# Banded attention with two feed-forward blocks: VectorE's maxima and softmax sums as one run at the head of a step

## The chip, the cores and the metric

One core of a Trainium2 chip runs the whole program. The metric is device time in microseconds for one execution. The kernel before takes 594.93 us (median of three runs, 594.91 to 594.97). The profile is of one execution of 594.9 us; its span, from the first to the last instruction, is 593.1 us, so 1.8 us lie around it.

## The reference

Two batches of 8 heads, 768 positions, head width 64; then two feed-forward blocks on 1536 tokens.

```python
def _attn_ref(q, k, v, n_global, n_local):
    scores = scale * np.matmul(q, k.transpose(0, 1, 3, 2))
    keep = is_global | is_local            # the first 8 keys, and the last 96
    scores = np.where(keep, scores - slope * dist, -1e9)
    a = np.exp(scores - max(scores)); a = a / (a.sum(-1) + 1e-9)
    return np.matmul(a, v)

x = attn_out.transpose(0, 2, 1, 3).reshape(B * S, H * D)
x = (((x @ w1) * (x @ w2)) @ w3) @ w_out
x = ((x @ w_a) * (x @ w_b)) @ w_out2
```

## The kernel before

Attention works on **blocks** (tiles) of 128 queries: 12 of them, t = 0 to 11, six for each batch. A block's keys are its own 128 and the 128 before it; the first 32 columns of the older keys are overwritten by the batch's first keys (the global ones). A block has four units of two heads, so there are 48 units, u = 4t + c. The first batch (t < 6) multiplies the keys as they are; the second (t from 6) splits keys and queries into a rounded part and a remainder: `ks` holds both parts of the keys, `qa` and `qb` those of the queries.

The order of every engine is written by hand, one **step** after another (`band_attention`, the `while` loop). Each engine works its list strictly in order. In step u stand:

- TensorE: the scores of units u and u+1 (even u; L429 in the first batch, L446 in the second), the transposition of an older unit's probabilities (L509, unit u-5, from step 16 unit u-6), the product with the values (L545; from step 16 four units at once, in the steps with u % 4 == 2), and behind these a share of the first feed-forward block (`filler`, L827 to L829).
- ScalarE: the exponentials of unit u-2 (L481), the copy of the transposed probabilities out of PSUM (L511), a block's output rounded (`store_x`, L520), the rounded keys of a later block (`band_high`, L387), and the conversion of weights (L92, L93, L118).
- VectorE: two fused passes over the scores of unit u-1, which add the bias and find the maximum (`band_max`, L463), the sums of unit u-3 (`band_norm`: an addition L492 and a reciprocal L494; from unit 16 for two units at once, in even steps), the remainder of a block's output (`store_x_low`, L527), the copy of the global keys into the block's keys (`band_global`, L413; in the first block of a batch L411 sets them aside), the remainders of the keys and of the queries of a later block (`band_low`, L399 and L402), and the weight conversion (L97, L101, L105 in one step, L127 in the next).
- GpSimd: the division by the sums (`band_norm`, L498, two instructions for each unit, released by the reciprocal) and the rounded queries of a later block (`band_high`, L388, which writes `qa`; L402 reads it).

Block work has fixed steps. For block t: L388 and L387 in step 4t-4, L399 and L402 in step 4t-3, L413 in step 4t+3. The scores of block t+1, from step 4t+4 on, read the keys that L413 writes.

Inside a step the VectorE work comes as generators (`turns`), and `feed` takes one instruction from each in turn until all are empty. Up to step 5 it first empties the generators of attention and only then starts the weight pieces. A stage that is no generator (L413, L388, L387, L520) issues its instructions where the list of turns is built, so ahead of the first maximum. A share of feed-forward work is given to each step by a count (`spent`), not by time: a step that lasts longer gets no more of it.

After attention (from about 125 us) the feed-forward blocks run to the end; the change touches nothing of them.

Of the kernel before, what the change touches and what calls it, by code (L numbers as in the profile page):

```python
# [31 lines left out]
class Emitter:  # L32
# [519 lines left out]
    def band_attention(self, filler):  # L552

        self.v, self.qs, self.sp, self.sm, self.pt, self.pv = ({} for _ in range(6))
        self.kq = dict(enumerate(self.kq01))
        self.ks = self.const.tile([P, 3, self.H, P], F32R, name=self.name("ks"))
        self.globs = self.const.tile([P, self.H, MAX_GLOBAL], F32, name=self.name("globs"))
        C = self.C
        nt = self.B * self.NB
        nu = nt * C  # L560
        self.patient = True
        masks = self.band_masks()
        self.feed_load(1, self.nc.scalar)
        next(masks)

        self.nc.vector.tensor_copy(out=self.nf, in_=self.ni.bitcast(U32))
        next(masks)
        block_stages = (
            (0, self.band_load_v), (C - 1, self.band_global), (-3, self.band_low), (-4, self.band_high), (-6, self.band_load),
        )  # L570
        early = sorted((C * t + lag, t, n) for t in range(nt) for n, (lag, _) in enumerate(block_stages) if C * t + lag < 0)
        for _, t, n in early:
            if t and n != len(block_stages) - 1:
                for _ in block_stages[n][1](t) or ():
                    pass
        spent = 0.0
        turned = valued = 0
        stores = {}
        u = -1
        while self.stored < nt:  # L580
            u += 1
            self.step = u
            at = lambda lag, stage: stage(u - lag) if 0 <= u - lag < nu else None
            at(0, self.band_scores)
            at(2, self.band_exp)
            while turned < min(nu, u - 4 if u < 16 else u - 5):
                self.band_turn(turned)
                turned += 1


            while valued < min(nu, u - 5 if u < 16 else u - 6) and (u < self.pairs_from or u % 4 == 2):
                self.band_values(valued)
                valued += 1
                if valued % C == 0:
                    for n, stage in enumerate((self.store_x, self.store_x_low, self.set_stored)):
                        stores.setdefault(u + n, []).append((stage, valued // C - 1))
            turns = [at(1, self.band_max), at(3, self.band_norm)]
            turns += [stage(t) for stage, t in stores.pop(u, ())]
            for lag, stage in block_stages:
                t, c = divmod(u - lag, C)  # L600
                if c == 0 and 0 <= t < nt:
                    turns.append(stage(t))
            self.feed([x for x in turns if x])
            if u:
                next(masks, None)
            for _ in range(2):
                if spent < 0.85 * (u - 14) - 0.15 * max(u - 38, 0):
                    spent += next(filler)
        self.patient = False
# [1131 lines left out]
```

## Time and profile before

| | us |
|---|---|
| median of the runs | 594.93 |
| profiled execution | 594.9 |
| its span | 593.1 |
| TensorE busy | 578.7 (98%) |
| VectorE busy | 459.7 (78%) |
| ScalarE busy | 376.5 (63%) |
| GpSimd busy | 186.9 (32%) |
| mean granted TensorE clock | 0.996 |

The shares are means over the whole span. The change lies between about 13 us (step 6) and 112 us (the last steps), so the views below are of that stretch: the busy time by stretches, the waits, and the timeline, whose rows give start, duration, engine, line, what is written from what, and in brackets the idle time before an instruction with what ended it. The views by windows give, for a stretch, the busy time of PE (TensorE's matmuls), PEld (its weight loads), DVE (VectorE), ACT (ScalarE) and POOL (GpSimd), in this order, and behind them the granted clock (1.00 is 2.4 GHz, 0.50 is 1.2 GHz). A busy time of TensorE of 100% means that matmul follows matmul. Start-to-start times show how fast an engine really takes its instructions: VectorE's maxima last 0.41 us each but start 0.34 us apart.

### The profile page before, as it was taken

The numbers are of one execution on the slowest core, as the hardware profiler recorded it, in microseconds if no ns is written. First come the engines' busy times: TensorE is split into PE (matmuls) and PEld (weight loads), VectorE is DVE, ScalarE is ACT, GpSimd is POOL, SyncE is SP. The second block draws the span as 40 slices with busy tenths as digits, with TensorE's granted clock in tenths as the row PEclk, the third lists the DMA queues.
The fourth block names the chain that finished last, engine by engine and source line by source line (L and its number), as shares of the span: only waits on it lengthen the run. The fifth ranks groups of instructions, "written<-read, shape, count | busy, mean of one in ns | idle before, by whom it ended". The sixth has DMA issues, their size and how long they took to land.

```text
span 593.1 us, 10332 instructions
## 1 busy us (share of the span) xinstructions
PE 578.7 (98%) x3620; PEld 504.9 (85%) x3620; DVE 459.7 (78%) x957; ACT 376.5 (63%) x818; POOL 186.9 (32%) x246
## 2 busy tenths in 40 slices
PE   6899999999999999999999999999999999999996
PEld 4589987888888888888899888888888888889996
DVE  6898979449969878777999677777777789984781
ACT  5999889747847756667564444444444465795830
POOL 5756746400231130321702022222222221564500
PEclk9899999999999999999999999999999999999999
DMA  8999973425899424896703122122220258999931
GB/s 229 282 251 234 204 196 101 143 75 175 223 221 272 137 72 106 190 198 110 106 1 143 36 72 72 35 72 72 71 72 1 71 147 221 237 143 189 199 95 57
DMA packets 33548, 82.02 MB, mean 138 GB/s; under 512 B 3792, under 2 KB 11472, under 8 KB 33488
## 3 DMA queue, kind: packets, MB, share of 16 engines
q1 hardware_dynamic: 20560, 57.42, 32.6%
q0 software_dynamic: 12352, 23.07, 23.0%
q10 hardware_dynamic: 576, 0.79, 0.5%
q8 instruction: 30, 0.49, 0.4%
q14 instruction: 30, 0.25, 0.1%
HBM read 55.05 MB, written 3.15 MB: 98 GB/s over the span
## 4 chain that ended last, share of the span: by engine, by line
PE 88%; ACT 5%; DVE 2%; issue 2%; POOL 1%; DMA 1%; SPq 0%; ACTq 0%; DVEq 0%; POOLq 0%
PE ab_band L1173 33%; PE o_band L1173 16%; PE y_band L1173 10%; PE ab_band L827 5%; PE ab_band L828 5%; PE ab_band L829 5%; PE wfp_band L262 2%; PE wfp_band L263 2%; PE wfp_band L264 2%; PE pv_band L545 2%; ACT s_band L481 2%; PE pt_band L509 2%; PE sp_band L446 1%; DMA kq<-in_kq_dram 1%; ACT pt_band L511 1%
## 5 line engine op out<-in xcount | busy, mean ns | idle before, releaser
L1173 PE MATMUL ab_band<-y_band,ws_band 128*128 128x512 f32 (+1 forms) x576 | 110.1, 337 | 0.0
L1173 PEld LDWEIGHTS ab_band<-y_band,ws_band 128*128 128x128 f32 x576 | 91.0, 190 | 12.0
L498 POOL TENSOR_SCALAR s_band<-s_band,z_band 128x256 f32<-128x256 f32 (+1 forms) x96 | 57.8, 617 | 35.0 <-DVE ks_band L413 11.2
L827 PE MATMUL ab_band<-xh_band,w_band 128*128 128x512 f32 (+1 forms) x168 | 63.1, 376 | 0.0
L829 PE MATMUL ab_band<-xh_band,w_band 128*128 128x512 f32 (+1 forms) x168 | 60.3, 359 | 0.0
L828 PE MATMUL ab_band<-xl_band,w_band 128*128 128x512 f32 (+1 forms) x168 | 60.3, 359 | 0.0
L1173 PE MATMUL o_band<-wo_band,gs_band 128*128 128x256 f32 (+1 forms) x360 | 59.1, 326 | 0.0
L1173 PE MATMUL y_band<-gs_band,wf_band 128*128 128x512 f32 (+1 forms) x336 | 58.4, 336 | 0.0
L1173 PEld LDWEIGHTS o_band<-wo_band,gs_band 128*128 128x128 f32 x360 | 53.0, 190 | 5.9
L1173 PEld LDWEIGHTS y_band<-gs_band,wf_band 128*128 128x128 f32 x336 | 51.8, 190 | 6.6
L1173 PE MATMUL ab_band<-y_band,wa_band 128*128 128x512 f32 (+1 forms) x288 | 56.4, 338 | 0.0
L1173 PEld LDWEIGHTS ab_band<-y_band,wa_band 128*128 128x128 f32 x288 | 46.0, 190 | 6.1
L93 ACT ACTIVATE raw_band<-raw_band 128x512 int32<-128x512 uint32 x74 | 49.7, 672 | 0.0
L481 ACT ACTIVATE s_band<-s_band,m_band 128x256 f32<-128x256 f32 (+1 forms) x96 | 46.8, 497 | 1.3 <-DVE m_band L463 1.3
L1375 ACT COPY p_band<-ab_band 128x512 f32<-128x512 f32 (+1 forms) x48 | 22.0, 483 | 33.0 <-PE ab_band L1173 33.0
L1018 POOL TENSOR_TENSOR sf_band<-gb_band 128x256 f32<-128x256 f32 x12 | 10.4, 863 | 97.2 <-DVE gb_band L105 75.3
L1376 DVE TENSOR_TENSOR u_band<-ab_band,u_band 128x512 f32<-128x512 f32 (+1 forms) x24 | 13.3, 554 | 33.1 <-PE ab_band L1173 32.7
L463 DVE CUSTOM_DVE_ANT_0 s_band<-sp_band,bias_band 128x256 f32<-128x256 f32 (+1 forms) x96 | 37.1, 389 | 0.5 <-PE sp_band L429 0.4
L827 PEld LDWEIGHTS ab_band<-xh_band,w_band 128*128 128x128 f32 x168 | 31.6, 188 | 5.8 <-issue 1.4
L829 PEld LDWEIGHTS ab_band<-xh_band,w_band 128*128 128x128 f32 x168 | 31.6, 188 | 4.9
L118 ACT CAST w_band<-g_band 128x512 fp32r<-128x512 f32 x36 | 22.6, 627 | 20.6 <-DVE g_band L105 20.5
L1416 POOL DMA_DIRECT2D ga_band<-ga_band x24 | 23.9, 1288 | 37.1 <-DVE gs_band L1311 24.4
(208 smaller groups left out, 1374.4 us busy)
## 6 DMA issues: line engine op xcount, KB each, us to landing
raw_band<-in_moe_w_dram SPq DMA_DIRECT2D x29, 512.0 KB, 6.6
raw_band<-in_moe_w_out_dram SPq DMA_DIRECT2D x20, 512.0 KB, 4.3
raw_band<-in_moe_w_b_dram SPq DMA_DIRECT2D x12, 512.0 KB, 3.5
raw_band<-in_moe_w_a_dram SPq DMA_DIRECT2D x12, 512.0 KB, 4.0
ga_band<-ga_band POOLq DMA_DIRECT2D x24, 256.0 KB, 6.9
v_band<-in_v_dram SPq DMA_DIRECT2D x12, 256.0 KB, 8.1
kd_band<-in_kq_dram SPq DMA_DIRECT2D x12, 256.0 KB, 8.5
qd_band<-in_kq_dram SPq DMA_DIRECT2D x12, 256.0 KB, 8.4
```

What stands on the lines that cost most here:

```text
L93: nc.scalar.activation(out=low, in_=low.bitcast(U32), func=AF.Copy, scale=2.0**-29)
L118: nc.scalar.mul(hi, g, sign) if sign < 0 else nc.scalar.copy(out=hi, in_=g)
L463: nc.vector.tensor_tensor_reduce(out=s[:, j, lo:], in0=sp[:, j, lo:], in1=bias[:, 2 * c + j, :], scale=-self.scale, scalar=FLT_MAX, op0=AL ...
L481: nc.scalar.activation(out=s[:, j, lo:], in_=s[:, j, lo:], func=AF.Exp, bias=m[:, j : j + 1], scale=-1.0, accum_out=z[:, j : j + 1],)
L498: nc.gpsimd.tensor_scalar(out=s[:, j, lo:], in0=s[:, j, lo:], scalar1=z[:, j : j + 1], scalar2=1.0, op0=ALU.mult, op1=ALU.mult)
L827: nc.tensor.matmul(p, wl, xh, start=(c == 0), stop=False)
L828: nc.tensor.matmul(p, wh, xl, start=False, stop=False)
L829: nc.tensor.matmul(p, wh, xh, start=False, stop=(c == self.C - 1))
L1173: self.nc.tensor.matmul(bank, wt, xt, start=start and i == n == 0, stop=stop and n == 2 and i == len(terms) - 1, skip_group_check=more,)
L1375: copy = lambda out: nc.scalar.copy(out=out, in_=bank)
L1376: plus = lambda t: nc.vector.tensor_tensor(out=t, in0=bank, in1=t, op=ALU.add)
L1416: add = lambda out, a: nc.gpsimd.dma_start(out, a, accum_op=ALU.add)
```

## The change

From step 6 on, the loop empties the two generators `band_max` and `band_norm` before the list of turns goes on: one instruction of each in turn, until both are done. What stood between them follows: the block stages' own instructions (L413, L411, L388, L387, L520), then the remaining generators and the weight pieces in turn, as before. Steps 0 to 5 stay as they are, and so do the numbers of instructions. TensorE, ScalarE and the DMA queue keep their orders word for word; VectorE and GpSimd change theirs.

```diff
-            turns = [at(1, self.band_max), at(3, self.band_norm)]
-            turns += [stage(t) for stage, t in stores.pop(u, ())]
+            first = [x for x in (at(1, self.band_max), at(3, self.band_norm)) if x]
+            while first and u > 5:
+                for turn in list(first):
+                    if next(turn, first) is first:
+                        first.remove(turn)
+            turns = first + [stage(t) for stage, t in stores.pop(u, ())]
             for lag, stage in block_stages:
```

Lines from 598 on stand four lines lower in the changed kernel (L837 is L841 there).

VectorE, step 11, before (each maximum is two rows, the pass and the reading of its result; `globs` are the global keys, `kq` the keys of block 2):

```order
L105 ISA g_band_467<-raw_band_299,g_band_467 128x1024
L413 COPY kq_band_274<-globs_band_222 128x4x32
L463 ISA s_band_537,m_band_538<-sp_band_481,bias_band_230 128x256
L463 ISA m_band_538 128x1
L492 TENSOR_SCALAR z_band_491<-z_band_491 128x2
L463 ISA s_band_537,m_band_538<-sp_band_481,bias_band_230 128x256
L463 ISA m_band_538 128x1
L494 RECIPROCAL z_band_491<-z_band_491 128x2
```

and now:

```order
L105 ISA g_band_475<-raw_band_388,g_band_475 128x1024
L463 ISA s_band_536,m_band_537<-sp_band_481,bias_band_230 128x256
L463 ISA m_band_537 128x1
L492 TENSOR_SCALAR z_band_491<-z_band_491 128x2
L463 ISA s_band_536,m_band_537<-sp_band_481,bias_band_230 128x256
L463 ISA m_band_537 128x1
L494 RECIPROCAL z_band_491<-z_band_491 128x2
L413 COPY kq_band_274<-globs_band_222 128x4x32
```

The copy of the global keys has moved from ahead of the step's four softmax instructions to behind them.

VectorE, step 37 (the remainders for block 10), before, from its first maximum:

```order
L463 ISA s_band_1558,m_band_1559<-sp_band_1496,bias_band_230 128x256
L463 ISA m_band_1559 128x1
L399 TENSOR_TENSOR ks_band_221<-kd_band_1458,ks_band_221 64x1024
L97 TENSOR_SCALAR g_band_1525<-g_band_1525 128x512
L463 ISA s_band_1558,m_band_1559<-sp_band_1496,bias_band_230 128x256
L463 ISA m_band_1559 128x1
L402 TENSOR_TENSOR qb_band_1521<-qd_band_1459,qa_band_1520 128x1024
```

and now:

```order
L463 ISA s_band_1558,m_band_1559<-sp_band_1496,bias_band_230 128x256
L463 ISA m_band_1559 128x1
L463 ISA s_band_1558,m_band_1559<-sp_band_1496,bias_band_230 128x256
L463 ISA m_band_1559 128x1
L399 TENSOR_TENSOR ks_band_221<-kd_band_1468,ks_band_221 64x1024
L97 TENSOR_SCALAR g_band_1535<-g_band_1535 128x512
L402 TENSOR_TENSOR qb_band_1531<-qd_band_1469,qa_band_1530 128x1024
```

The second maximum has moved ahead of L399, and nothing but L97 is left between L399 and L402.

GpSimd, step 36, before (L388 writes the rounded queries of block 10, each L498 row is the division of one unit):

```order
L388 TENSOR_SCALAR qa_band_1520<-qd_band_1459 128x1024
L498 TENSOR_SCALAR s_band_1414<-s_band_1414,z_band_1437 128x256 x2
L498 TENSOR_SCALAR s_band_1464<-s_band_1464,z_band_1437 128x256 x2
L498 TENSOR_SCALAR s_band_1490<-s_band_1490,z_band_1506 128x256 x2
L498 TENSOR_SCALAR s_band_1528<-s_band_1528,z_band_1506 128x256 x2
```

and now:

```order
L498 TENSOR_SCALAR s_band_1414<-s_band_1414,z_band_1437 128x256 x2
L498 TENSOR_SCALAR s_band_1456<-s_band_1456,z_band_1437 128x256 x2
L388 TENSOR_SCALAR qa_band_1530<-qd_band_1469 128x1024
L498 TENSOR_SCALAR s_band_1489<-s_band_1489,z_band_1506 128x256 x2
L498 TENSOR_SCALAR s_band_1516<-s_band_1516,z_band_1506 128x256 x2
```

L388 has moved from ahead of its step's four divisions to behind them. The same happens in steps 20, 24, 28, 32 and 40.

## Rows read from the trace of the kernel before

**Rows 1.** Windows: start:end, length, busy us (instructions) by engine, clock, DMA share, GB/s.

```profile
125.00:588.00 463.00, 463.00 (x2591) 406.16 (x2589) 362.38 (x593) 272.65 (x503) 115.54 (x124) 1.00 0.51 123
```

**Rows 2.** Waits of TensorE: for whom, us in total, times, longest.

```profile
PE pv_band L545 <- ACT pt_band L511: 1.7, 2, 1.4
...
PE sp_band L446 <- DVE ks_band L413: 1.0, 1, 1.0
```

**Rows 3.** Timeline, steps 10 to 12: VectorE, TensorE's weight load (PEld), ScalarE.

```profile
22.42 0.43 DVE L97 TENSOR_SCALAR g_band<-g_band 128x512 int32<-128x512 int32 x1 [0.19 <-ACT g_band L92]
...
24.93 0.22 DVE L413 COPY kq_band<-globs_band 128x128 f32<-128x128 f32 x1
25.07 0.42 DVE L463 CUSTOM_DVE_ANT_0 s_band<-sp_band,bias_band 128x256 f32<-128x256 f32 x1
...
25.21 0.37 PEld L429 LDWEIGHTS sp_band<-kq_band,kq_band 64*128 64x128 f32 x4 [0.29 <-DVE kq_band L413]
...
25.90 0.40 DVE L463 CUSTOM_DVE_ANT_0 s_band<-sp_band,bias_band 128x256 f32<-128x256 f32 x1
...
28.08 0.58 ACT L511 COPY pt_band<-pt_band 128x512 f32<-128x512 f32 x1 [0.67 <-PE pt_band L509]
```

**Rows 4.** Windows inside steps 12 to 14, columns as in the first group.

```profile
26.00:29.00 3.00, 3.00 (x22) 2.12 (x20) 2.06 (x10) 2.33 (x7) 2.36 (x4) 0.50 1.06 273
30.00:33.00 3.00, 3.00 (x38) 2.29 (x34) 2.86 (x14) 3.00 (x12) 1.68 (x3) 1.00 1.08 222
```

**Rows 5.** Timeline, steps 35 and 36: copy for block 8, divisions, scores.

```profile
80.29 0.27 DVE L413 CAST ks_band<-globs_band 128x256 fp32r<-128x256 f32 x1
...
80.57 1.84 POOL L498 TENSOR_SCALAR s_band<-s_band,z_band 128x256 f32<-128x256 f32 x4 [4.03 <-DVE ks_band L413]
...
81.61 0.36 PE L446 MATMUL sp_band<-ks_band,qb_band 128*128 128x256 f32 x1
```

**Rows 6.** Timeline, step 24: GpSimd's L388 beside VectorE's L492.

```profile
55.77 1.05 POOL L388 TENSOR_SCALAR qa_band<-qd_band 128x1024 fp32r<-128x1024 f32 x1
...
55.81 1.04 DVE L492 TENSOR_SCALAR z_band<-z_band 128x4 f32<-128x4 f32 x1
```

**Rows 7.** Timeline, steps 36 and 37: VectorE, and ScalarE's rounded keys.

```profile
82.68 0.17 DVE L494 RECIPROCAL z_band<-z_band 128x4 f32<-128x4 f32 x1
...
83.89 1.05 ACT L387 CAST ks_band<-kd_band 128x1024 fp32r<-128x1024 f32 x1
...
84.97 1.34 DVE L399 TENSOR_TENSOR ks_band<-kd_band,ks_band 64x1024 fp32r<-64x1024 f32 x1 [1.81 <-ACT ks_band L387]
...
86.69 0.42 DVE L463 CUSTOM_DVE_ANT_0 s_band<-sp_band,bias_band 128x256 f32<-128x256 f32 x1
...
87.03 1.22 DVE L402 TENSOR_TENSOR qb_band<-qd_band,qa_band 128x1024 fp32r<-128x1024 f32 x1
```

**Rows 8.** Timeline, steps 38 to 40: VectorE, GpSimd, and the scores of block 10.

```profile
90.96 0.17 DVE L494 RECIPROCAL z_band<-z_band 128x4 f32<-128x4 f32 x1
91.05 0.26 DVE L413 CAST ks_band<-globs_band 128x256 fp32r<-128x256 f32 x1
...
91.33 0.48 POOL L498 TENSOR_SCALAR s_band<-s_band,z_band 128x256 f32<-128x256 f32 x1 [6.08 <-DVE ks_band L413]
...
91.37 0.39 PE L446 MATMUL sp_band<-ks_band,qb_band 128*128 128x256 f32 x1 [1.00 <-DVE ks_band L413]
```

**Rows 9.** Timeline, steps 40 to 44: VectorE, ScalarE, and the scores of block 11.

```profile
93.74 0.91 DVE L492 TENSOR_SCALAR z_band<-z_band 128x4 f32<-128x4 f32 x1
...
94.15 1.04 ACT L387 CAST ks_band<-kd_band 128x1024 fp32r<-128x1024 f32 x1
...
97.66 1.21 DVE L402 TENSOR_TENSOR qb_band<-qd_band,qa_band 128x1024 fp32r<-128x1024 f32 x1
...
101.07 0.26 DVE L413 CAST ks_band<-globs_band 128x256 fp32r<-128x256 f32 x1
...
101.48 0.36 PE L446 MATMUL sp_band<-ks_band,qb_band 128*128 128x256 f32 x1
```

## The prediction

> **What bounds the kernel now.** I looked first at TensorE by stretches. From 125 us to the tail it is busy in all 463 of 463 us [rows 1], so a delay that TensorE takes in the attention stage before that is handed to the end in full, and a wait that it loses there is won in full. That makes its own waits the second view. Before 125 us they are few: for ScalarE's copies of transposed probabilities (1.7 us in two waits), and 1.0 us once for VectorE's copy of the global keys, L413 [rows 2]. The third view is the timeline around those places, to see which engine ends the wait. ScalarE and TensorE both run almost without a gap from 30 us (3.00 of 3.00 us busy each) [rows 4], so a change of VectorE's order can win only what stands in those waits, and can lose wherever it makes an instruction late that TensorE needs.
>
> TensorE needs three things of VectorE here: the maxima (through the exponentials), L413 before the scores of the next block, and L402 three steps ahead of them. The change moves the first forward and the other two back.
>
> **What the maxima bring.** In the timeline no exponential that TensorE depends on stands on the path at a place where the maximum ends its wait; the two waits for ScalarE are for copies that stand in an unbroken ScalarE list. Earlier maxima and reciprocals therefore end no wait of TensorE by themselves. I take 0 for them; if some of the 1.7 us went with them, the sum falls by that at most.
>
> **L413 in the first batch.** In step 11 TensorE's scores start at 25.21, and the weight load ahead of them waited 0.29 us for L413 [rows 3]. L413 is the end of a VectorE chain that ScalarE releases: L97 starts at 22.42 when L92 is done. In the new order the whole run of step 11 comes ahead of L413: two passes, the addition and the reciprocal, from 25.07 to 25.90, 0.83 us. One pass and the reciprocal of step 10, half of such a run (0.42 us), leave the chain, since they now run before L97's wait. L413 comes 0.83 - 0.42 = 0.41 us later, the scores too, and ScalarE's copy at 28.08, which waits 0.67 us for TensorE already [rows 3], waits as much more. After it ScalarE has no gap that could take it up. **Term A: +0.41 us**, between 0 (if VectorE comes earlier into step 10) and 0.83. The other copies of this batch have room: they stand over 1.5 us ahead of the scores that read them, an estimate from the steps' lengths.
>
> **L413 in the second batch.** The run there is two passes (start to start 0.34 us each, as from 86.69 to 87.03 [rows 7]): 0.68 us in front of L413. In step 35 L413 ends at 80.56 and the scores start at 81.61 [rows 5]: 1.05 us of room, so nothing. In step 39 it ends the 1.00 us wait at 91.37 [rows 8], and in step 43 it ends at 101.33, with scores at 101.48 [rows 9]: there every delay goes through.
>
> **L402 behind L388.** This is the larger part. GpSimd's L388 (1.05 us) now follows the four divisions of its step, and L402 reads what it writes. VectorE, in order, stands still at L402 until then, and behind L402 are queued L101, L105, the next maxima and L413.
>
> For block 10: the reciprocal of step 36 is at 82.68 [rows 7]; a division starts 0.37 us after its reciprocal (90.96 to 91.33 [rows 8]), so at 83.05; four last 1.84 us [rows 5], to 84.89; L388 to 85.94. L399 becomes ready at 84.97, with ScalarE's L387 [rows 7]. The two engines block each other: an L492, an instruction of some 0.17 us, lasted 1.04 us, to the end of an L388 that had begun just before it [rows 6]. So L399 starts at 85.94 instead of 84.97. From L399 to the second pass it took 1.72 us; that pass now lies ahead, so L402 starts at 85.94 + 1.72 = 87.66, not 87.03. If L399 comes first, L388 ends at about 84.97 + 1.34 + 1.05 = 87.36: L402 0.33 us late instead of 0.63. The Trainium skill (SBUF — State Buffer, Who interferes with whom) says that whichever of the two issues first has the shared ports for its whole instruction and the other blocks fully; by that rule L388, 0.08 us ahead, wins, which gives the 0.63, and this trace's 1.04 us agrees.
>
> From L402 to L413 it is 4.02 us now (87.03 to 91.05 [rows 7, 8]), and 4.70 with two passes more: L413 at 92.36, 1.31 us late. TensorE was waiting for it, so **term B: +1.31 us** (1.01 with L399 first).
>
> For block 11 all that follows from these scores is 1.31 us later: L387 ends at 95.19 + 1.31 = 96.50 [rows 9]. VectorE, which has two passes less behind L413, is 1.31 - 0.68 = 0.63 us later, and its L492, which was blocked (0.91 us), is free (0.17): the reciprocal follows it at 93.74 + 0.63 + 0.17 + 0.34 = about 94.9, the divisions run from 95.2 to 97.1. L399 gets in between two of them, at about 96.6, to 97.9; one division (0.46) and L388 (1.05) follow, and L402 starts at 99.4. Without the stall it would be 97.66 + 1.31 = 98.97. L413 was 3.41 us behind L402 and is now 4.09: at 103.5. The scores start 0.32 us after it (91.05 to 91.37 [rows 8]), at 103.8; TensorE is ready at 101.48 + 1.31 = 102.79. **Term C: +1.0 us**, 0.6 with no stall at L402, 1.4 if L388 is again first.
>
> Blocks 6 to 9 get the same stall, but TensorE does not wait for L413 there now; I take 0 and up to 0.8 us if it uses up the 1.05 us of room [rows 5].
>
> Sum: 0.41 + 1.31 + 1.0 = 2.7 us. On the profiled execution, 594.9 us, which is the median of the runs, that is **597.6 us**.
>
> **Rivals.**
>
> *Only the copy is late.* The free L492 (0.91 to 0.17 [rows 9], 1.04 to 0.17 [rows 6]) lets the divisions begin so early, or L399 comes so late, that L388 is done when L402 is due. Then step 39 costs 0.68 - 0.34 (the pass that ran between L399 and L402 fills L399's wait of 1.81 us [rows 7]), 0.34 us, and step 43 about 0.1: 594.9 + 0.41 + 0.34 + 0.1 = 595.7. For it: in steps 36 and 37 the race is decided by 0.08 us. Against: it must be won in both of the last blocks.
>
> *Not slower: VectorE gets ahead.* L413 of step 39 comes early enough that the 1.00 us wait goes in spite of the two passes: 594.9 + 0.41 - 1.00 = 594.3. VectorE must then reach step 38 about 1.7 us sooner, and so L399 must start by 83.3; it waits for ScalarE's L387, which starts at 83.89 [rows 7] in a list that is not changed. That speaks against it.
>
> *The clock falls once more.* From 26 to 29 us the granted clock was 0.50, 1.2 GHz, after TensorE had waited for ScalarE and for L413; in 3 us it finished 22 matmuls, against 38 at 2.4 GHz [rows 4]. A second stretch like it, behind the new waits, costs about 3 x (1 - 22/38) = 1.3 us: 598.9. Against it: the wait of 1.00 us at 91.37 [rows 8] is in a span whose mean granted clock is 0.996, which leaves room for hardly another such stretch. The Trainium skill (TensorE: Matmul & The Clock Gate, HAM oscillation — how this bites in real kernels) describes waits that bring the clock down again and again; in this trace that has happened once in the stage.
>
> **How the numbers follow.** The forecast 597.6 has a chance of 0.56, with a range of its own from 596.4 (both stalls at their small ends and term A near 0.2) to 599.0 (blocks 8 and 9 lose 0.8 as well, term C at 1.4). Only the copy late, 595.7: 0.25. Not slower, 594.3: 0.08. The clock, 598.9: 0.07. The rest, 0.04, lies above. The range from 595.2 to 599.4 takes in all but the third case, a little of the second and the rest. About 0.2%, 1.2 us, is what a measurement of this kernel can tell from no change, so slower begins at 596.1: 0.67 from the first, fourth and last cases and a little of the second. Within it lies most of the second case and half of the third, 0.27; faster keeps 0.06.
>
> **What would show it.** In the trace of the changed kernel: the weight load of the scores in step 12 waits about 0.7 us for L413; L402 waits for GpSimd's L388 in steps 37 and 41; L492 in the steps with L388 lasts 0.17 us; TensorE waits for L413 some 2.3 us before the scores of block 10 and 1 us before those of block 11; from 125 us on all is the same, 2.7 us later. I am wrong if L402 shows no wait (then the second case), if TensorE's wait at block 10 is gone (the third), or if ScalarE shows new gaps for L118, which follows L105 and comes late with it.

## The result, and the profile after

The changed kernel takes 598.45 us (median of four runs, 597.84 to 598.67), the kernel before 594.92 us beside it; the ratio is 1.0062, with a 95% interval from 1.0049 to 1.0074. The same program, measured once more beside three of the experiments, took 597.03 us against 594.63 us: 1.0042 (1.0028 to 1.0056). So it is 2.4 to 3.5 us slower. The forecast was 597.6 us, 2.7 us slower. All medians, ratios and intervals here are of fast runs alone, and a ratio is estimated from the single runs, so it need not be the quotient of the two medians.

The profiled execution after took 597.84 us, with a span of 596.0 us, 2.9 us more than before. In the feed-forward blocks nothing changed, against [rows 1]. The two other stretches are the one that ran at the lower clock before [rows 4], and a new one. Windows of the changed kernel, columns as in [rows 1]:

```profile
125.00:588.00 463.00, 463.00 (x2581) 405.85 (x2580) 362.56 (x594) 273.18 (x504) 115.50 (x124) 1.00 0.52 124
...
26.00:29.00 3.00, 2.82 (x32) 2.30 (x32) 2.56 (x14) 2.85 (x8) 2.41 (x5) 1.00 1.07 266
...
93.40:96.40 3.00, 3.00 (x13) 2.99 (x14) 2.71 (x13) 1.20 (x6) 2.37 (x5) 0.50 0.00 0
```

TensorE is full from 125 us on in both kernels, so all of the loss arises in attention. The stretch at 26 us has the full clock here, and a stretch at 93 us has the granted clock 0.50: the lower of the two levels, 1.2 GHz, with 13 matmuls in 3 us.

The waits of TensorE between 17 and 112 us, against [rows 2], and the first row of VectorE's own waits there:

```profile
PE sp_band L446 <- DVE ks_band L413: 2.4, 2, 2.1
PE pv_band L545 <- ACT pt_band L511: 1.9, 3, 0.7
PE sp_band L429 <- DVE kq_band L413: 0.5, 1, 0.5
```

```profile
DVE qb_band L402 <- POOL qa_band L388: 4.0, 3, 1.7
```

The waits for ScalarE are nearly what they were (1.9 us for 1.7); the wait for L413 has grown from 1.0 to 2.1 us and has two companions, and VectorE stands at L402 behind L388, which it never did before.

The timeline of the changed kernel around blocks 9 to 11, to be read beside [rows 5, 7 to 9]: start, duration, engine, line, what is written from what, and the idle time ahead with what ended it.

```profile
79.48 1.23 DVE L402 TENSOR_TENSOR qb_band<-qd_band,qa_band 128x1024 fp32r<-128x1024 f32 x1 [0.94 <-POOL qa_band L388]
...
83.94 0.17 DVE L494 RECIPROCAL z_band<-z_band 128x4 f32<-128x4 f32 x1
...
85.79 1.42 DVE L399 TENSOR_TENSOR ks_band<-kd_band,ks_band 64x1024 fp32r<-64x1024 f32 x1 [1.02 <-ACT ks_band L387]
87.24 1.17 DVE L97 TENSOR_SCALAR g_band<-g_band 128x512 int32<-128x512 int32 x1
88.33 1.21 DVE L402 TENSOR_TENSOR qb_band<-qd_band,qa_band 128x1024 fp32r<-128x1024 f32 x1
...
92.99 0.29 DVE L413 CAST ks_band<-globs_band 128x256 fp32r<-128x256 f32 x1
...
97.92 1.65 DVE L399 TENSOR_TENSOR ks_band<-kd_band,ks_band 64x1024 fp32r<-64x1024 f32 x1 [1.80 <-ACT ks_band L387]
...
99.94 1.22 DVE L402 TENSOR_TENSOR qb_band<-qd_band,qa_band 128x1024 fp32r<-128x1024 f32 x1
```

```profile
84.30 1.84 POOL L498 TENSOR_SCALAR s_band<-s_band,z_band 128x256 f32<-128x256 f32 x4 [0.63 <-PE pt_band L509]
86.11 2.02 POOL L388 TENSOR_SCALAR qa_band<-qd_band 128x1024 fp32r<-128x1024 f32 x1
```

```profile
93.33 0.58 PE L446 MATMUL sp_band<-ks_band,qb_band 128*128 128x256 f32 x1 [2.06 <-DVE ks_band L413]
...
104.86 0.28 PE L446 MATMUL sp_band<-ks_band,qb_band 128*128 128x256 f32 x1
```

The chain at block 10 reads so. L402 of block 9, at 79.48, has waited for its own L388. VectorE is late from there, and its reciprocal of step 36 stands at 83.94 instead of 82.68. GpSimd's divisions follow at 84.30, and L388 gets its turn at 86.11. By then L399 is under way; L388 and L399 overlap, L388 lasts 2.02 us instead of 1.05 and holds up L97 (1.17 us, 0.43 before). So L402 starts at 88.33 instead of 87.03, L413 at 92.99 instead of 91.05, and the scores of block 10 at 93.33 instead of 91.37.

Where the time went, as the starts of the scores against the kernel before, in us (positive is later), worked out from the starts of L429 and L446 in the two traces:

| place | start before | changed kernel against it | what was added since the row above |
|---|---|---|---|
| step 16 | 35.5 | +0.03 | |
| step 36, block 9 | 81.61 | +0.87 | 0.84, from the stalls of blocks 7 to 9 and L413 behind two more passes |
| step 40, block 10 | 91.37 | +1.97 | 1.10, the longer wait for L413 |
| step 42 | 96.08 | +3.47 | 1.50, behind that wait, at the lower clock |
| step 44, block 11 | 101.48 | +3.38 | -0.09 |
| end of TensorE's work | | +2.79 | -0.59 |

The last 0.6 us came back in one place. Behind the scores of block 11 eight transpositions took 1.51 us before and take 1.07 us now: their weight loads waited 0.23 and 0.26 us for GpSimd's divisions before, and wait for none now. The transposition rows, of the kernel before and of the changed one:

```profile
102.57 1.51 PE L509 MATMUL pt_band<-ident,s_band 128*128 128x128 f32 x8
```

```profile
105.86 1.07 PE L509 MATMUL pt_band<-ident,s_band 128*128 128x128 f32 x8
```

### The profile page after: what moved, and what is told of

The parts are those of the page before. It is cut to its first block, busy times and chain, and to the rows that moved or that the text cites. A ratio compares the mean times of both kernels' runs of the same rounds, so it can differ in the third digit from the quotient of the medians.

```text
span 596.0 us, 10336 instructions
## 1 busy us (share of the span) xinstructions
PE 580.4 (97%) x3620; PEld 507.0 (85%) x3620; DVE 457.3 (77%) x957; ACT 376.7 (63%) x818; POOL 181.8 (30%) x246
## 4 chain that ended last, share of the span: by engine, by line
PE 86%; ACT 5%; DVE 4%; issue 2%; POOL 1%; DMA 1%; POOLq 0%; SPq 0%; ACTq 0%; DVEq 0%
PE ab_band L1177 33%; PE o_band L1177 16%; PE y_band L1177 10%; PE ab_band L831 5%; PE ab_band L833 4%; PE ab_band L832 4%; PE wfp_band L263 2%; PE wfp_band L264 2%; PE wfp_band L262 2%; PE pv_band L545 2%; ACT s_band L481 2%; PE pt_band L509 2%; DVE s_band L463 1%; PE sp_band L446 1%; ACT pt_band L511 1%
## 5 line engine op out<-in xcount | busy, mean ns | idle before, releaser
L498 POOL TENSOR_SCALAR s_band<-s_band,z_band 128x256 f32<-128x256 f32 (+1 forms) x96 | 51.7, 555 | 45.5 <-ACT s_band L481 11.0
L118 ACT CAST w_band<-g_band 128x512 fp32r<-128x512 f32 x36 | 22.5, 626 | 21.2 <-DVE g_band L105 21.1
L832 PEld LDWEIGHTS ab_band<-xl_band,w_band 128*128 128x128 f32 x168 | 31.8, 190 | 4.3
```

The source lines that it names most:

```text
L118: nc.scalar.mul(hi, g, sign) if sign < 0 else nc.scalar.copy(out=hi, in_=g)
L498: nc.gpsimd.tensor_scalar(out=s[:, j, lo:], in0=s[:, j, lo:], scalar1=z[:, j : j + 1], scalar2=1.0, op0=ALU.mult, op1=ALU.mult)
L832: nc.tensor.matmul(p, wh, xl, start=False, stop=False)
```

## The experiments

Theory at the start: the loss comes from L388 behind the divisions (the stall at L402) and from L413 behind two more passes. Rivals: only L413; the run itself; the clock. Eleven kernels were run, in three sets, each set beside the kernel before. The table gives their times, and for the profiled execution of each the same offsets as above.

| kernel | median, us | ratio to before (95%) | 35 us | block 9 | block 10 | step 42 | end | wait at block 10 |
|---|---|---|---|---|---|---|---|---|
| changed (first set of runs) | 598.45 | 1.0062 (1.0049 to 1.0074) | +0.03 | +0.87 | +1.97 | +3.47 | +2.79 | 2.06 |
| e1 L413 ahead, L388 behind | 596.28 | 1.0026 (1.0015 to 1.0037) | -0.26 | -0.13 | +1.01 | +2.48 | +1.80 | 2.10 |
| e2 L388 ahead, L413 behind | 594.67 | 1.0003 (0.9993 to 1.0013) | -1.25 | -1.22 | -0.78 | -0.79 | -1.45 | 1.44 |
| e3 both ahead | 594.10 | 0.9999 (0.9988 to 1.0009) | -0.22 | -0.23 | -0.58 | -0.58 | -0.74 | 0.65 |
| e4 from step 20 on | 596.95 | 1.0036 (1.0022 to 1.0050) | -0.81 | +0.20 | +1.32 | +2.90 | +2.23 | 2.09 |
| e5 in steps 6 to 19 | 595.01 | 1.0015 (1.0000 to 1.0029) | +0.15 | +0.15 | +0.19 | +0.19 | +0.17 | 1.04 |
| e6 L388 ahead, L413 a step sooner | 594.96 | 1.0010 (0.9993 to 1.0026) | -1.53 | -0.09 | -0.41 | -0.41 | -0.53 | 0.68 |
| e7 changed, wait filled | 597.26 | 1.0040 (1.0026 to 1.0055) | +0.10 | +0.96 | +2.09 | +2.09 | +2.30 | 0.66 |
| e8 changed, again | 597.03 | 1.0042 (1.0028 to 1.0056) | +1.15 | +1.84 | +2.97 | +4.53 | +3.86 | 2.12 |
| e9 L413 ahead of the run, sooner | 594.44 | 0.9990 (0.9975 to 1.0005) | -0.33 | -0.27 | -1.45 | -0.70 | -0.57 | none |
| e10 L388 behind in step 36 alone | 597.65 | 1.0047 (1.0030 to 1.0064) | -1.19 | +0.22 | +1.32 | +2.88 | +2.21 | 2.10 |
| e11 before, L413 seven times | 600.10 | 1.0087 (1.0072 to 1.0102) | +0.46 | +0.46 | +3.68 | +6.20 | +5.58 | 4.22 |

The column at 35 us differs by up to 2.7 us between executions, also between those whose order is the same up to there (before and e4: 0.81 us; the changed kernel and e8: 1.12 us). So effects of the second batch are read as differences between columns of one row. Each row is one execution. How far such differences repeat can be seen where an order was run more than once: from 35 us to the scores of block 10 the new order loses 1.94, 2.13, 1.82 and 1.99 us (changed, e4, e8, e7), and the old order, in e5, differs from the kernel before by 0.04 us.

The profiled execution of the kernel before is not its usual case. It has the stretch at the lower clock at 26 us, and a mean granted clock of 0.996. Of the 71 executions of that kernel beside the three sets, 56 have a mean of 0.998 or more, with a median of 594.52 us, and the other 15 have one of 595.59 us. This is one reason why the offsets at the end, of e2 and e3 above all, say less than 0 where the ratios say 1.

### Which of the moved instructions costs

Three kernels put one or both of the stages back ahead of the run. The edit of e1; e2 has `(self.band_high,)` there, e3 both:

```diff
             first = [x for x in (at(1, self.band_max), at(3, self.band_norm)) if x]
+            ahead = (self.band_global,)
+            for lag, stage in block_stages:
+                t, c = divmod(u - lag, C)
+                if u > 5 and stage in ahead and c == 0 and 0 <= t < nt:
+                    stage(t)
             while first and u > 5:
...
-                if c == 0 and 0 <= t < nt:
+                if (u <= 5 or stage not in ahead) and c == 0 and 0 <= t < nt:
                     turns.append(stage(t))
```

Expected of e1:

> The changed kernel with one part undone: the copies of the global keys (L413, L411) stand ahead of the run again; GpSimd's L388 stays behind its step's divisions. Theory (both parts cost, L413 by two passes, L402 by its wait for L388): the copy of step 35 ends 0.68 us sooner, so the 0.36 us wait at the scores of block 9 goes, and of the 2.06 us wait at block 10 about 0.7 goes too; L402 still waits 0.9 to 1.7 us for L388. About 595.8 to 596.4 us, less by 1.5 where the shorter wait no longer brings the clock down at 93 us. Rival (only the late copy costs): the time of the kernel before, 594.9, and no wait at L402 that matters.

Expected of e2:

> The other part undone: GpSimd's L388 stands ahead of its step's divisions again; the copies of the global keys stay behind the run. Theory: no wait at L402, the scores of block 9 do not wait, those of block 10 wait about 1.0 + 0.3 us, those of block 11 hardly: 595.1 to 595.6 us. Rival (only the late copy costs, L388 is hidden): close to the changed kernel, 597.5 or more, with a wait of some 2 us at block 10.

Expected of e3:

> Both parts undone: L413, L411 and L388 ahead of the run; what is left of the change is that maxima and sums come before the weight pieces, L527 and L399. Theory: nothing is left that costs, and the second pass of step 37 falls into L399's wait for ScalarE: 594.4 to 595.0 us. Rival (the order of the maxima against the weight pieces costs by itself, through ScalarE's L118): 595.5 or more with new ScalarE waits for L105.

Measured: with L388 ahead (e2, e3) the loss is gone, 1.0003 and 0.9999. The 594.67 us of e2 are below the 595.1 to 595.6 expected. With L413 ahead alone (e1) 1.0026 remains, and the wait at block 10 is 2.10 us, where some 1.4 were expected: the wait at block 9 is gone, so that TensorE stands there sooner by about as much as L413 does. From 35 us to the scores of block 10 (column "block 10" minus column "35 us") the four kernels make a square:

| | L413 ahead of the run | L413 behind |
|---|---|---|
| L388 ahead of the divisions | -0.36 (e3) | +0.47 (e2) |
| L388 behind the divisions | +1.27 (e1) | +1.94 (changed) |

The rows differ by 1.63 and 1.47, the columns by 0.83 and 0.67: within the 0.3 us by which such numbers repeat the two costs add, and the run alone brings 0.36 us, hardly more than that. L388's place is worth twice L413's. Two rows of e2, VectorE's L402 and the scores of block 10:

```profile
85.56 1.22 DVE L402 TENSOR_TENSOR qb_band<-qd_band,qa_band 128x1024 fp32r<-128x1024 f32 x1
```

```profile
90.58 0.39 PE L446 MATMUL sp_band<-ks_band,qb_band 128*128 128x256 f32 x1 [1.44 <-DVE ks_band L413]
```

L402 waits for nothing, and the wait of 1.44 us is the old one of 1.00 us [rows 8] and the 0.47 us of the square, but for 0.03.

### The early steps and the late ones

e4 has `while first and u > 19` in place of `u > 5`, e5 `5 < u < 20`, and e8 is the changed kernel as it is.

Expected of e4:

> The change from step 20 on alone; steps 6 to 19 as in the kernel before. The profile of the changed kernel shows TensorE no later than before at 35 us, though the copy of step 11 was waited for 0.2 us longer, and a stretch at 1.2 GHz gone at 26 us. Theory A (the early part costs nothing in the end): as the changed kernel, 597.8 to 598.7 us. Theory B (the early part costs 0.4 us, which the clock happened to give back in the profiled execution): 0.4 us less than the changed kernel in most executions.

Expected of e5:

> The new order only in steps 6 to 19, the old one from step 20 on. Theory (term A): the scores of step 12 wait 0.7 us for L413 instead of 0.29, TensorE gets nothing back before 125 us, +0.4 us, ratio 1.0007. Rival: the early part is decided by when the granted clock leaves 0.50 before 30 us, not by L413: then scores at 35 us stand anywhere from -1.0 to +1.0 us against the kernel before, while the wait for L413 is 0.7 us in any case; the median then tells nothing of term A.

Expected of e8:

> The changed kernel itself, beside the three others on the same chip. If its two halves are independent, its loss over the kernel before is that of steps 6 to 19 alone plus that of steps 20 on alone (0.0036 of the time, 2.1 us, in the run before this one): about 2.1 + 0.4 = 2.5 us if term A is right, ratio 1.0043; 3.5 us, ratio 1.006, if the early steps cost 1.4 us. Rival: the halves are not independent, and the sum of the two parts differs from the whole by over 1 us.

Measured: steps from 20 on alone give 1.0036, the early steps alone 1.0015, with an interval that touches 1; the whole, beside e5, 1.0042. Within the intervals the parts add. The 596.95 us of e4 are below both of its theories: the first runs of the changed kernel, from which these were reckoned, took more than e8. In e5 nothing is lost after 35 us (0.15 to 0.19), in e4 everything is: from -0.81 to +2.23, 3.0 us.

For the early steps the trace tells more than the times. The weight load of the scores of step 12, in the changed kernel:

```profile
26.18 0.37 PEld L429 LDWEIGHTS sp_band<-kq_band,kq_band 64*128 64x128 f32 x4 [0.73 <-DVE kq_band L413]
```

It has waited 0.73 us for L413, in e5 0.78 and in e8 0.77 us. In the kernel before it was 0.29 us [rows 3], in e4, which has the old order there, 0.33 us. The wait of 0.4 us more is there in each of the three. But the offset at 35 us doesn't follow it: +0.03, +0.15 and +1.15 us. In the first two the clock around 26 us is at its upper level, while in e8 and in the kernel before a stretch of 3.4 us there is at the lower one. That decides more than L413 does, as the rival in the expectation of e5 had it.

What the new order does to L413 there can be read apart from this, from L97, which ScalarE releases, to L413. In the kernel before that is 2.51 us (22.42 to 24.93 [rows 3]), in e4 and e11, with the same order, 2.51 and 2.50 us. In the changed kernel it is 2.94 us, in e5 2.98 and in e8 2.97 us, 0.43 to 0.47 us more. VectorE in the changed kernel:

```profile
22.98 0.43 DVE L97 TENSOR_SCALAR g_band<-g_band 128x512 int32<-128x512 int32 x1 [0.15 <-ACT g_band L92]
...
25.92 0.20 DVE L413 COPY kq_band<-globs_band 128x128 f32<-128x128 f32 x1
```

But L97 is 0.56 us later there too, and so the scores of step 12 start 0.97 us later (26.18 for 25.21). That goes back to TensorE: its matmuls of step 8 ran at half the pace, four in 0.42 us instead of 0.22, ScalarE's copy L511 behind them starts at 19.41 instead of 18.88, and L92, which L97 waits for, at 22.25 instead of 21.65. The scores of step 10 start at 21.61 instead of 20.16. A row of the kernel before and one of the changed kernel, four matmuls each:

```profile
16.57 0.39 PE L429 MATMUL sp_band<-kq_band 64*128 64x128 f32 x4
```

```profile
17.27 0.64 PE L429 MATMUL sp_band<-kq_band 64*128 64x128 f32 x4
```

The view gives the granted clock as 1.00 in both. It is so in e5 and e8 as well (step 10 at 21.65 and 20.94), but not in e2 and e10, which have the order of the changed kernel up to there (19.91 and 19.95). So the order alone does not decide it; what does was not tried.

### How the stall at block 10 grew

In e10 L388 stands ahead of the divisions in all steps but 36 (the edit of e2, with block 10 taken out).

> The new order of maxima, sums and L413, with L388 ahead of its step's divisions everywhere but in step 36 (block 10), where it stays behind them as in the changed kernel. It tests how the stall at L402 came to be larger than the 0.63 us of the prediction. Theory: most of it was carried over from the same stalls of blocks 7 to 9, which made VectorE's reciprocal of step 36, and so the divisions and L388, 1.3 us late. Without them the scores of block 10, counted from those of 35 us, come 0.47 us (L388 ahead everywhere) + 0.63 = 1.1 us later than in the kernel before, with a wait of about 2.0 us for L413; median 595.2 to 595.8, ratio 1.001 to 1.002 (1.003 if the granted clock falls behind the wait). Rival: the stall at block 10 is a matter of its own step alone (L399 keeps GpSimd's L388 busy twice as long): then they come 1.9 us later, as in the changed kernel, and the ratio is 1.004.

From the scores of block 9 to those of block 10 it loses 1.10 us (0.22 to 1.32), as the theory said, with a wait of 2.10 us. From 35 us on, as the theory counted, it is 2.51 us, of which 1.43 were lost near 50 us (last section). Rows of e10, GpSimd's L388 and VectorE:

```profile
85.16 1.06 POOL L388 TENSOR_SCALAR qa_band<-qd_band 128x1024 fp32r<-128x1024 f32 x1
```

```profile
83.00 0.17 DVE L494 RECIPROCAL z_band<-z_band 128x4 f32<-128x4 f32 x1
...
85.19 2.10 DVE L399 TENSOR_TENSOR ks_band<-kd_band,ks_band 64x1024 fp32r<-64x1024 f32 x1 [1.36 <-ACT ks_band L387]
...
87.67 1.22 DVE L402 TENSOR_TENSOR qb_band<-qd_band,qa_band 128x1024 fp32r<-128x1024 f32 x1
```

Here the stall of block 10 is alone, and it runs as the prediction had it: L388 0.03 us ahead of L399, L399 held for 2.10 us, L402 at 87.67. The reciprocal is at 83.00, within 0.1 us of where it belongs (82.68 before and the 0.22 us of this execution). In the changed kernel it is at 83.94: the rest of that delay is the stalls of the blocks ahead. The Trainium skill (SBUF — State Buffer, Who interferes with whom) says that the one of the two that issues first holds the shared ports for its whole instruction; these rows agree nearly: L399 ends at 87.29, 1.07 us after L388's end at 86.22, where undisturbed it takes 1.34 us [rows 7], so that 0.3 us of it at most ran beside L388.

The median of e10 is higher than expected. In the profiled execution two things add to the stall: the clock falls behind the wait, and 1.43 us are lost near 50 us, in steps whose order is that of e2 (last section). Seven of the ten executions have a mean granted clock of 0.994 or less, where the profiled one, with one stretch at the lower clock, has 0.997.

### The clock

In all profiled executions with a wait of 2.06 to 2.12 us at block 10 (the changed kernel, e1, e4, e8, e10) the granted clock is 0.50 for 3.4 us behind it; in those with 0.65 to 1.44 us it stays. Two experiments ask whether the wait does it, and what it costs. e7 is the changed kernel with twelve more matmuls in that wait, whose results the scores overwrite; its lines from L430 on stand four lower, L450 is L446 and L438 the added matmul:

```diff
             own, prev = t % 3, (t - 1) % 3
+            for n in range(12 if u == 40 else 0):
+                nc.tensor.matmul(
+                    sp[0][:, 0, :], self.qs[t][0][:, 0, :], self.qs[t][0][:, 0:2, :], start=True, stop=True
+                )
             for r in range(2):
```

> The changed kernel with 12 more matmuls of 256 columns on TensorE just ahead of the scores of block 10, into a bank that the scores then overwrite (0.14 us each, 1.7 us in all, of the 2.06 us that TensorE waits there). Theory: the granted clock of 0.50 from 93.2 to 96.6 us came because TensorE stood still before it; with the wait filled the clock stays, the eight score matmuls take 1.1 instead of 2.1 us, and the end comes 1.3 to 1.5 us sooner than in the changed kernel, ratio 1.002 to 1.004 over the kernel before. Rival: the clock falls there whatever TensorE does (the stretch after block 10 is what brings it down), or it is not that stretch that costs: the end is that of the changed kernel or up to 0.3 us later, ratio 1.005 to 1.0065.

e11 is the kernel before with a longer wait: in `band_global` the copy is issued seven times for block 9 (the same values each time). Its lines from L413 on stand one lower: L414 is L413, L447 is L446.

> The kernel before, with L413 of step 39 issued seven times instead of once (0.17 us each start to start, 1.0 us in all). Its wait of TensorE at block 10 grows from 1.0 to about 2.0 us, with nothing else changed. Theory: the fall of the granted clock to 0.50 in the changed kernel belongs to a stand of TensorE of some 2 us there, whatever brought it: the clock falls here too, the eight score matmuls take 2.1 us, and the end comes 1.0 us (wait) + 0.5 to 1.4 us (clock) later, ratio 1.0025 to 1.004. Rival: it takes more of the changed kernel than the wait: the clock stays, the end comes 0.4 to 1.0 us later, ratio 1.0007 to 1.0017.

TensorE's rows in e7, its waits for L413, and the window behind the scores of block 10:

```profile
91.12 1.68 PE L438 MATMUL sp_band<-qa_band 128*128 128x256 f32 x12
93.46 0.39 PE L450 MATMUL sp_band<-ks_band,qb_band 128*128 128x256 f32 x1 [0.66 <-DVE ks_band L413]
...
104.33 0.35 PE L450 MATMUL sp_band<-ks_band,qb_band 128*128 128x256 f32 x1 [0.68 <-DVE ks_band L413]
```

```profile
93.46:96.46 3.00, 3.00 (x20) 2.69 (x21) 2.79 (x13) 2.48 (x7) 2.37 (x5) 1.00 0.00 0
```

The clock stays, with 20 matmuls in 3 us instead of 13, and step 42 is 1.38 us earlier than in the changed kernel. So the wait brought the clock down. But the end comes only 0.49 us earlier in the profiled execution (2.30 against 2.79), where 1.3 to 1.5 were expected, and the medians, 597.26 and 597.03, show no difference. The rest went at block 11. L413 starts there at nearly the same time in both, 103.89 in e7 and 104.02 in the changed kernel. In e7 TensorE is ready 0.68 us before its scores of 104.33 and waits; in the changed kernel the slow stretch has made it late, and it does not wait. VectorE in e7:

```profile
99.81 1.22 DVE L402 TENSOR_TENSOR qb_band<-qd_band,qa_band 128x1024 fp32r<-128x1024 f32 x1 [0.94 <-POOL qa_band L388]
```

At full clock block 11 has the stall at L402 too; in the changed kernel it has none (99.94, above), since its L399 waited 1.80 us for ScalarE's keys, and L388 was done meanwhile.

Other executions have no trace, but their mean granted clock is on record. It is 0.999 in the profiled executions without a stretch at the lower clock, 0.996 or 0.997 in those with one of 3.4 us, and 0.994 in e8, which has two. Three of the nine executions of e8 have 0.999 or 1.0, so hardly such a stretch; they took 596.91 to 597.03 us, and the median of all nine is 597.03. Three of e4 have 0.998 or 0.999 and took 596.93 to 596.97 us; the profiled one, in which the clock fell, took 597.06 us. So the clock does not fall in every execution of the new order, and most of the loss is there without it.

e11 missed its size: the wait became 4.22 us, not 2.0, because the copies did not keep their 0.17 us beside GpSimd's work. Rows of e11, VectorE, GpSimd and TensorE, and two windows:

```profile
91.50 3.49 DVE L414 CAST ks_band<-globs_band 128x256 fp32r<-128x256 f32 x7
```

```profile
92.82 0.98 POOL L499 TENSOR_SCALAR s_band<-s_band,z_band 128x256 f32<-128x256 f32 x2
93.78 1.07 POOL L388 TENSOR_SCALAR qa_band<-qd_band 128x1024 fp32r<-128x1024 f32 x1
```

```profile
95.05 0.58 PE L447 MATMUL sp_band<-ks_band,qb_band 128*128 128x256 f32 x1 [4.22 <-DVE ks_band L414]
```

```profile
95.10:98.10 3.00, 3.00 (x13) 3.00 (x14) 3.00 (x15) 1.23 (x5) 0.15 (x1) 0.50 0.00 0
98.10:100.60 2.50, 2.50 (x8) 1.82 (x8) 0.97 (x2) 2.50 (x4) 1.69 (x4) 0.50 0.00 0
```

The lower clock is there without anything else of the change, and lasts twice as long; from block 10 to step 42 it costs 2.5 us (3.68 to 6.20). So it takes no more than a long stand of TensorE at this place. Whether a stand of 2.0 us would do it in the old order, e11 doesn't tell.

### Two versions that were to gain

Both keep the run and have L388 ahead. e6 moves L413 to step 4t+2, behind the run (`C - 2` in `block_stages`); e9 has L413 ahead of the run, from step 38 on in step 4t+2.

Expected of e6:

> The maxima and sums as one run, L388 ahead of the divisions, and L413 one step sooner (step 4t+2, behind the run). Theory: what TensorE waits for at block 10 (0.65 us with L413 ahead of the run of step 39) is only VectorE's place in its list, so the wait goes, and with it 0.6 to 1.0 us against the kernel before: 593.6 to 594.0, ratio 0.998 to 0.999. Rival: L413 now waits for TensorE's last scores of its own block and holds up VectorE's weight pieces behind it, or the wait moves to ScalarE's copies: no gain, ratio 1.000 to 1.002.

Expected of e9:

> Maxima and sums as one run, L388 ahead of the divisions, L413 ahead of the run, and for blocks 9 and 10 ahead of the run of the step before (38 and 42), right behind the weight pieces. Theory: TensorE's wait at block 10 (0.65 us with L413 ahead of step 39's run) is VectorE's place in its list, and four softmax instructions (0.85 us) leave it: the wait is under 0.1 us, the end 0.6 us before that of the kernel with L413 ahead of step 39's run, ratio 0.997 to 0.9995. Rival: TensorE then waits at block 10 for something else that is ready at the same time (ScalarE's copies, GpSimd's divisions), or loses the gain in the steps behind, as the runs so far lost parts of what they had won: ratio 0.9995 to 1.001.

For neither is a gain over the kernel before shown: 1.0010 (0.9993 to 1.0026) and 0.9990 (0.9975 to 1.0005). In e6 the place behind the run of step 38 is the same as that ahead of the run of step 39, and the wait is e3's. In e9 the wait at block 10 is gone and 1.18 us are won there; 0.75 us are lost again in the next two steps. The transposition behind the scores, in e9:

```profile
91.44 0.89 PE L509 MATMUL pt_band<-ident,s_band 128*128 128x128 f32 x4 [0.30 <-POOL s_band L498]
```

It waits for the first of its two divisions, and its four matmuls take 0.89 us instead of 0.60, since the second division (91.36 to 91.84) ends while they run. The divisions follow VectorE's reciprocal, and that is as late as before: what L413 no longer holds up, the divisions do.

## Why the prediction was right, point by point

**What bounds the kernel.** Right: nothing changes after 125 us, and the end moved by what the scores of the last blocks moved.

**Earlier maxima bring nothing.** Nearly: with both stages back in their places (e3) the run wins 0.36 us at block 10, and 0.5 us by the end (-0.22 to -0.74). e9, which takes the wait at block 10 away altogether, wins no more by the end (-0.33 to -0.57). The list of TensorE's waits in the prediction left out those for GpSimd's divisions, 0.9 us in two in the kernel before; the larger one, 0.75 us at 18.16, is not there in the changed kernel, whose TensorE comes to that transposition 0.53 us later (18.69).

**Term A, +0.41 us.** Right in its step: the weight load waits 0.73 us, 0.44 more than before, and L413 takes 0.43 us longer from L97. That TensorE keeps this loss to the end could not be shown: executions of one order differ by over 1 us at 35 us, with the pace of step 8 and with where the lower clock lies. In the profiled execution the offset is 1.45 us at step 10 and 0.97 at step 12, and at 35 us it is 0.03: the stretch at 26 us runs at the upper clock there, which the kernel before lacked.

**Blocks 6 to 9: 0, up to 0.8 us.** This step failed in size: 0.84 us in the changed kernel, 1.01 in e4, 0.69 in e8. The prediction had VectorE's delay in blocks 7 to 9 too small. It followed the stall of one block from an undisturbed VectorE ("the reciprocal of step 36 is at 82.68") and asked only whether L413's 1.05 us of room were used up. But VectorE does not recover between the blocks: it comes out of block 9's L402 1.17 us late (79.48, against 78.31 before), the reciprocal and the divisions follow, and the next L388 starts as much later than the forecast's 84.89 (86.11). The room of 1.05 us was used up: L413 ahead of block 9 is 1.84 us later than before (82.13 for 80.29 [rows 5]), 1.17 from the stall and 0.67 from the two passes, and the scores wait 0.36 us for it. VectorE and TensorE in the changed kernel:

```profile
82.13 0.29 DVE L413 CAST ks_band<-globs_band 128x256 fp32r<-128x256 f32 x1
```

```profile
82.47 0.39 PE L446 MATMUL sp_band<-ks_band,qb_band 128*128 128x256 f32 x1 [0.36 <-DVE ks_band L413]
```

It takes both: e1 has the stalls and L413 ahead of the run, and loses 0.13 us from 35 us to block 9. VectorE's waits at L402 in e1:

```profile
DVE qb_band L402 <- POOL qa_band L388: 5.4, 4, 1.6
```

**Term B, +1.31 us.** Right in mechanism and nearly in size: 1.10 us from block 9 to block 10 in the changed kernel, and 1.10 in e10, where the stall is alone and every step of the working can be seen (L388 first, L399 blocked). That L402 starts at 87.67 there, for 87.66 forecast, is chance: 0.22 us of it is the offset of this execution, so the stall costs 0.42 us and not 0.63, since L399 was not held for the whole of L388. In the changed kernel it came about in the other order, L399 first and L97 blocked, for which the prediction had 1.01 us. It is so in e4, e7 and e8 too, which carry the same delay into block 10 (L399 0.33 to 0.36 us ahead of L388).

**Term C, +1.0 us.** Absent in the changed kernel (-0.09), present at full clock: in e7 L402 of block 11 starts at 99.81 (99.4 forecast) after a stall, L413 at 103.89 (103.5), and the scores are 0.8 us later (+2.09 to +2.85).

**The clock, given 0.07.** Here the argument was wrong: that the clock stayed after a wait of 1.00 us was taken from a wait half as long as the one that the forecast itself expected (2.3 us). The clock fell in every profiled execution with a wait of over 2 us, though by the mean clocks not in every execution. The size, 1.3 us, was near the 1.5 us by which step 42 came later. But the prediction added it to the whole sum, and it came in the place of term C: against e7 0.5 us of it is left at the end, and by the medians nothing. The Trainium skill (TensorE: Matmul & The Clock Gate, HAM oscillation — how this bites in real kernels) describes waits of TensorE that bring the clock down again and again; e7 agrees, where the clock stays with the wait filled.

That the sum of the profiled execution came out within 0.1 us (+2.79 for 2.7) is luck. Too little was forecast for blocks 7 to 9 (0 for 0.84) and for what follows block 10 (1.0 for term C, where 1.50 for the clock less 0.09 came). Too much was forecast for term A (0.41, where 0.03 is left at 35 us) and for term B (1.31 for 1.10), and 0.59 us came back behind block 11, which the prediction did not have. In e7, where the clock stays, the parts are 0.10 at 35 us, 0.86 for blocks 7 to 9, 1.13 for B, 0.76 for C and -0.55 behind block 11: the path of the prediction, with the carried delay in addition.

**Rivals.** "Only the copy is late" is what e2 is made to be; there L413 alone costs 0.47 us up to block 10, near the 0.34 forecast, and nothing in the median. "VectorE gets ahead" did not happen.

**What would show it.** The weight load's wait came (0.73). L402's waits came in three blocks, 7 to 9 and not the two that were named: in step 37 the delay stands in L97, and in step 41 it is missing. L492 lasts 0.35 us in step 36 and 0.23 in step 40, not quite 0.17. The wait at block 10 was 2.06 us for some 2.3, at block 11 none for 1. The gap of ScalarE's L118 came too, 0.57 us at 63.45, which I had named as a sign against me; TensorE's offset doesn't move by it (+0.09 us by step 30).

## What to carry to other kernels

An instruction that another engine is to read three steps later is not free to go behind the work of its step: follow who reads it, and who stands behind that reader. Follow such a stall through all the blocks that repeat it, not through one, since an engine that is nearly full carries the delay into the next. And when a forecast contains a wait of TensorE longer than any in the trace, the clock behind it belongs to the forecast, with the waits that it would replace, and not as a sum on top of them.

## What the runs showed of the hardware that was not expected

A half-clock stretch of 3.4 us delays the matmuls behind it by 1.5 us, but is worth only 0.5 us at the end where TensorE would soon have waited for VectorE anyway (profiled executions of e7 and the changed kernel; the medians show no difference).

VectorE's copy of 128x256 took 0.26 us alone and 0.50 us on average when it was issued seven times beside GpSimd's divisions and L388 (3.49 us for seven, e11).

The same order can run in two ways. e2 and e10 have the same instructions in the same order up to step 36, yet near 50 us GpSimd's three divisions took 3.56 us in one and 4.00 us in the other, and TensorE waited in the second alone. Three views, GpSimd in e2, GpSimd in e10 and TensorE in e10:

```profile
46.50 3.56 POOL L498 TENSOR_SCALAR s_band<-s_band,z_band 128x256 f32<-128x256 f32 x3
```

```profile
46.86 4.00 POOL L498 TENSOR_SCALAR s_band<-s_band,z_band 128x256 f32<-128x256 f32 x3
```

```profile
50.04 0.44 PE L509 MATMUL pt_band<-ident,s_band 128*128 128x128 f32 x2 [1.23 <-POOL s_band L498]
```

In the offsets that is 1.43 us, more than most of the effects under study. e6 lost as much at the same place. In e10 L388 started 0.36 us later than in e2, after a transfer that it waited for, and the traces show what hangs on it: in e2 the first division starts ahead of VectorE's L399 and takes 0.48 us, in e10 it starts behind L399 and takes 1.45 us, three times as long. GpSimd and VectorE in e2, then in e10:

```profile
46.50 0.48 POOL L498 TENSOR_SCALAR s_band<-s_band,z_band 128x256 f32<-128x256 f32 x1
```

```profile
46.68 1.37 DVE L399 TENSOR_TENSOR ks_band<-kd_band,ks_band 64x1024 fp32r<-64x1024 f32 x1
```

```profile
46.86 1.45 POOL L498 TENSOR_SCALAR s_band<-s_band,z_band 128x256 f32<-128x256 f32 x1
```

```profile
46.73 1.23 DVE L399 TENSOR_TENSOR ks_band<-kd_band,ks_band 64x1024 fp32r<-64x1024 f32 x1
```

In e6 the division starts behind L399 too, at 46.50 and 46.39. No run was made to move this start alone, so this stays a reading of three traces.
